# Two feed-forward layers behind clustered attention: the attention's score blocks cut into full 512-column banks, q and k kept in one tile, and the low parts of P and the weight conversions placed anew

## The chip, the cores and the metric

The kernel runs on one core of a Trainium2 chip. A core has five engines that run beside each other and wait for each other through semaphores: TensorE (PE, with PEld for its weight loads), VectorE (DVE), ScalarE (ACT), GpSimd (POOL) and SyncE (SP), which here issues all the transfers. Matmul results land in PSUM, which has eight banks; one bank holds 512 float32 columns on each of 128 partitions. The metric is the device time of one execution in microseconds (us).

## The reference

Attention over 2 batches, 8 heads, 768 positions, head size 64, in which a query sees only the keys of its own cluster; then two feed-forward layers on 1536 rows of 512, inner size 2048.

```python
q_assign = np.argmax(np.einsum('bhsd,hcd->bhsc', q_n, c_n), axis=-1)
k_assign = np.argmax(np.einsum('bhsd,hcd->bhsc', k_n, c_n), axis=-1)
mask = q_assign[:, :, :, None] == k_assign[:, :, None, :]
scores = scale * np.matmul(q, k.transpose(0, 1, 3, 2))
scores = np.where(mask, scores, -1000000000.0)
attn = softmax(scores)                 # max, exp, sum over the last axis
x = np.matmul(attn, v)                 # heads side by side: (1536, 512)
x = softplus(x @ moe_w_in) @ moe_w_out
x = leaky_relu(x @ moe2_w_in) @ moe2_w_out
```

The weights of the feed-forward layers arrive as float64.

## The kernel before, in words

There are 16 heads (8 of batch 0, then 8 of batch 1), and each head's 768 rows make six blocks of 128. Products are made in float16 with a high and a low part: A x B becomes hi x hi + hi x lo + lo x hi.

For one head, in order:

- `load`, `load_v` fetch q, k and v. `split` casts q and k to float16 (`nq`, `nk`), subtracts to get the low parts, and packs both into `n1`, which one transposing transfer turns into `t1`. `split_v` makes the high and low parts of v.
- `assign_mm`, `assign_el` find the cluster of each row: 24 matmuls of 16 columns, then five DVE instructions. ACT writes the one-hot clusters beside the high parts in `nq` and `nk`, and two transfers transpose these into `tq` and `tk`.
- `emit_s1` computes scores to find each query's maximum: per query block two matmuls of 384 columns, each into a bank of its own, and a DVE maximum over each (L250). `emit_m` joins the maxima, writes them into `nq` and has it transposed again (`tm`).
- `emit_s2` computes the scores once more, keys on the partitions, with the maximum subtracted: per key block `kt` two banks of 384 columns, two matmuls each, then the exponential on ACT (L277) into `p`, float32, 128 x 768. A low part `pl` of `p` is subtracted on POOL ("G") or DVE ("D"), as the table `PLO` says by group of heads and key block (L284). Where the table says "P", no low part is made.
- `emit_pv` multiplies P with v. Of a block with a low part, 18 short matmuls: 12 with the high part of P (L311, L312), 6 with `pl` (L316). Of a "P" block, six float32 matmuls (L298).
- `emit_norm` divides by the sum (DVE L345, L346, L348) and writes high and low parts, which are transposed into `xth`, `xtl`.

The feed-forward work (`moe1`) is a generator. Its `layer_in` takes 384 rows at a time and has 16 groups of 12 matmuls (L399); after each group ACT applies softplus twice (L377, L378) and DVE subtracts (L379). `layer_mid` has 16 steps of 12 matmuls (L412). `moe2` does the same with leaky relu, and `layer_out` (L431) ends it. From head 8 on, when the attention of batch 0 is done, `moe_steps` puts eight such steps beside each head.

Weights come in 64 pieces of 512 KB, 32 for each layer pair. `w_piece` issues the transfer into one of two `st` tiles and returns a function that converts it: three DVE instructions on the bits (L137, L140, L143), two on ACT (L147, L148), one on POOL (L149). `w_step` converts one piece and issues the next; it is called from the head loop and once for each step of `moe1`.

The order on each engine comes from the framework's scheduler, which is given a priority for every piece of code (`at_pri`: about the number of the head it belongs to, minus a lead). Every engine then runs its own list in that order. Softplus and the exponential need different ACT tables, so where they alternate, the list has an ACT_TABLE_LOAD in between.

Of the kernel before, what the change touches and what calls it, by code (L numbers as in the profile page):

```python
# [17 lines left out]
BIG = 32768.0  # L18
# [7 lines left out]
}  # L26
NQ_BUFS, NK_BUFS, V_BUFS = (3, 2), (2, 1), 3
# [4 lines left out]
HI = ("AA", "DA", "AA", "AA", "AA", "AA")  # L32
DUP = ("DD", "AA", "AA", "AA", "AA", "AA")
VLO = "GDGDDG"
PLO = ("GPGDGG", "GPGDGG", "GPGDGG", "GPGDGG", "GPPGPP", "GGDGGD")
# [11 lines left out]
def by_group(table, h):  # L47
    return table[min(h // 2, 4 + (h >= 12))]
# [3 lines left out]
def attn_moe_kernel(  # L52
# [50 lines left out]
    xt_h = [const.tile([128, KDM, SEQ], F16, name=f"xth{b}") for b in range(B)]  # L103
    xt_l = [const.tile([128, KDM, SEQ], F16, name=f"xtl{b}") for b in range(B)]
    def padded(bufs, name):
        n, late = sum(bufs), bufs[0]
        tiles = [(acon if i < late else ep).tile([128, C, 128], F16, name=f"{name}_{i}") for i in range(n)]
        return tiles, [tiles[h % n if h < H else (h - H) % late] for h in range(NH)]

    nqs, nq_of = padded(NQ_BUFS, "nq")  # L110
    nks, nk_of = padded(NK_BUFS, "nk")
# [67 lines left out]
    def split_v(h):  # L179
        vv, v2 = v_t.pop(h), v2s[h % V_BUFS]  # L180
        S.copy(out=v2[:, :, D:2 * D], in_=vv)
        ENG[by_group(VLO, h)].tensor_tensor(out=v2[:, :, 0:D], in0=vv, in1=v2[:, :, D:2 * D], op=ALU.subtract)

    def split(h):
        qk = ld_t.pop(h)
        nq, nk = nq_of[h], nk_of[h]
        n1 = atile([128, C, 4, D], F16, "n1", h)
        for t_, n_ in enumerate((nq, nk)):
            (S.copy if by_group(HI, h)[t_] == "A" else V.tensor_copy)(out=n_[:, :, 0:D], in_=qk[:, t_])
            G.tensor_tensor(out=n1[:, :, 1 + t_, :], in0=qk[:, t_], in1=n_[:, :, 0:D], op=ALU.subtract)  # L190
            (S.copy if by_group(DUP, h)[t_] == "A" else V.tensor_copy)(out=n1[:, :, 3 * t_, :], in_=n_[:, :, 0:D])
# [18 lines left out]
    def assign_el(h):  # L210
        nq, nk = nq_of[h], nk_of[h]
# [24 lines left out]
    def emit_s1(h, c):  # L236
        t, tk = tp2[h]
        if c == 0:
            mm_t[h] = atile([128, C, 2], F32, "mm", h)
        for j in range(2):  # L240
            bank = ring("s1", h)
            o = bank[:, 0:3 * 128].rearrange("p (c r) -> p c r", c=3)
            PE.matmul(  # L243
                out=o,
                lhsT=t[0:KS1, c, :],
                rhs=tk[0:KS1, 3 * j:3 * j + 3, :],
                start=True,
                stop=True,
            )
            V.reduce_max(out=mm_t[h][:, c, j:j + 1], in_=bank[:, 0:3 * 128], axis=AX)  # L250

    def emit_m(h):
        nq = nq_of[h]
# [13 lines left out]
    def emit_s2(h, kt):  # L267
        t1 = tp1[h].rearrange("p (c t) r -> p c t r", t=2)
        t2 = tp2[h][1]
        tqh = tpq[h]  # L270
        p = atile([128, 2, 384], F32, "p", h)
        for j in range(2):
            sp = ring("s2", h)[:, 0:384]
            o = sp.rearrange("p (c r) -> p c r", c=3)
            PE.matmul(out=o, lhsT=t1[:, kt, 1, :], rhs=t1[:, 3 * j:3 * j + 3, 0, :], start=True, stop=False)  # L275
            PE.matmul(out=o, lhsT=t2[0:KS2, kt, :], rhs=tqh[0:KS2, 3 * j:3 * j + 3, :], start=False, stop=True)  # L276
            S.activation(out=p[:, j, :], in_=sp, func=AF.Exp, scale=scale)  # L277
        pb = p.bitcast(BF16).rearrange("p a (r t) -> p a r t", t=2)[:, :, :, 1]
# [10 lines left out]
    def emit_pv(h, kt):  # L289
        v2 = v2s[h % V_BUFS]  # L290
        if kt == 0:
            x_t[h] = px.tile([128, 512], F32, tag="x", name="x")
        xps = x_t[h]
        p, pl = p_t.pop((h, kt))
        if pl is None:
            pf = p.rearrange("p a r -> p (a r)")
            for c in range(C):
                PE.matmul(  # L298
                    out=xps[:, c * XW:(c + 1) * XW],
                    lhsT=pf[:, c * 128:(c + 1) * 128],  # L300
                    rhs=v32s[h % V_BUFS][:, kt, :],
                    start=(kt == 0 and c == 0),
                    stop=False,
                )
            return
        pb = p.bitcast(BF16).rearrange("p a (r t) -> p (a r) t", t=2)[:, :, 1]
        pl = pl.rearrange("p a r -> p (a r)")
        for c in range(C):
            cs = slice(c * 128, (c + 1) * 128)
            o = xps[:, c * XW:(c + 1) * XW]  # L310
            PE.matmul(out=o, lhsT=pb[:, cs], rhs=v2[:, kt, D:2 * D + 1], start=(kt == 0 and c == 0), stop=False)  # L311
            PE.matmul(out=o[:, 0:D], lhsT=pb[:, cs], rhs=v2[:, kt, 0:D], start=False, stop=False)  # L312
        for c in range(C):
            cs = slice(c * 128, (c + 1) * 128)
            o = xps[:, c * XW:(c + 1) * XW]
            PE.matmul(out=o, lhsT=pl[:, cs], rhs=v2[:, kt, D:2 * D + 1], start=False, stop=False)  # L316
# [324 lines left out]
```

## Time and profile before

| | |
|---|---|
| median of 3 runs | 817.93 us (815.01 to 820.43) |
| the profiled execution | 823.73 us |
| its span, first to last instruction | 822.0 us |
| PE / PEld busy | 735.4 / 448.0 us |
| DVE / ACT / POOL busy | 413.3 / 386.2 / 228.4 us |
| mean granted TensorE clock | 0.962 of full speed |

Busy time of PE is not PE at its peak: matmuls are pipelined, and the profile's ends of them overlap. Where PE is full, the time from the start of one matmul to the start of the next is what counts.

### The profile page before, as it was taken

Reading aid. Unit: us, or ns where it says so; the run is one execution under the profiler, and the core shown is the slowest. Engines: PE = TensorE matmul, PEld = TensorE weight load, DVE = VectorE, ACT = ScalarE, POOL = GpSimd, SP = SyncE. Lnnn points to the kernel's source line nnn. Section 1 sums busy time; section 2 is a strip of 40 time slices with the busy share of each in tenths; the row PEclk is TensorE's granted clock in tenths of the full one; section 3 lists DMA queues with packets and bytes.
Section 4 is the critical chain, followed back from the end, with each engine's and each line's share of the span. In section 5 each row is a group of like instructions: output and inputs, shape, how many; then the busy total and the mean of one; then the engine's idle time right before and its main releaser. Section 6 shows DMA issues by size and latency. Waiting matters only on the chain.

```text
span 822.0 us, 14081 instructions
## 1 busy us (share of the span) xinstructions
PE 735.4 (89%) x5712; PEld 448.0 (55%) x5712; DVE 413.3 (50%) x790; ACT 386.2 (47%) x797; POOL 228.4 (28%) x192
## 2 busy tenths in 40 slices
PE   1688988798887999998979779999999999999998
PEld 1256656565554675665545446666644644644643
DVE  6899997889687764522778971211200210210210
ACT  3466656479798633497535641412411411411410
POOL 4266757645164443422434340000000000000000
PEclk9999988989879898999999999999999999999999
DMA  7976656685656463101455430000000000000000
GB/s 186 224 172 123 117 119 144 106 203 148 152 145 144 114 110 69 31 1 20 139 157 167 154 102 1 1 1 1 1 14 26 1 14 26 1 13 26 1 14 26
DMA packets 104881, 66.02 MB, mean 80 GB/s; under 512 B 90992, under 2 KB 95088, under 8 KB 104816
## 3 DMA queue, kind: packets, MB, share of 16 engines
q1 hardware_dynamic: 104816, 65.13, 33.2%
q8 instruction: 44, 0.72, 0.4%
q14 instruction: 21, 0.17, 0.1%
HBM read 43.02 MB, written 3.15 MB: 56 GB/s over the span
## 4 chain that ended last, share of the span: by engine, by line
PE 56%; DVE 18%; ACT 11%; DMA 10%; issue 3%; SPq 1%; POOL 0%; ACTq 0%; DVEq 0%; POOLq 0%
PE m L399 21%; PE m L431 15%; PE m L412 10%; DVE mm L250 4%; DVE wc L143 3%; DVE wc L140 3%; DMA st<-in_moe_w_in_dram 3%; DVE wc L137 2%; ACT L377 2%; ACT p L277 2%; PE x L298 2%; DMA tm<-nq 2%; DMA tk<-nk 2%; PE s L275 2%; PE s L243 1%
## 5 line engine op out<-in xcount | busy, mean ns | idle before, releaser
L379 DVE TENSOR_TENSOR g_l<-mr,g_h 128x384 f16<-128x384 f32 x128 | 77.1, 603 | 235.0 <-ACT mr L378 235.0
L284 POOL TENSOR_TENSOR pl<-p 128x768 f16<-128x768 f32 x56 | 89.2, 1599 | 83.1 <-ACT p L277 77.0
L250 DVE TENSOR_REDUCE mm<-s 128x1 f32<-128x384 f32 x160 | 85.5, 549 | 39.3 <-PE s L243 38.5
L377 ACT ACTIVATE g_h<-m 128x384 f16<-128x384 f32 x128 | 62.4, 488 | 88.7 <-PE m L399 88.2
L277 ACT ACTIVATE p<-s 128x384 f32<-128x384 f32 x160 | 75.7, 488 | 52.9 <-PE s L276 49.8
L399 PE MATMUL m<-xth,w_inh 128*128 128x384 f16 x256 | 85.0, 335 | 7.7 <-ACT mr L378 7.7
L412 PE MATMUL m<-g_h,w_outh 128*128 128x384 f16 x256 | 84.9, 332 | 7.7 <-DVE xtl L417 4.9
L412 PE MATMUL m<-g_l,w_outh 128*128 128x384 f16 x256 | 84.9, 332 | 3.7 <-DVE g_l L379 3.7
L399 PE MATMUL m<-xtl,w_inh 128*128 128x384 f16 x256 | 85.3, 334 | 0.0
L412 PE MATMUL m<-g_h,w_outl 128*128 128x384 f16 x256 | 84.9, 332 | 0.0
L399 PE MATMUL m<-xth,w_in2h 128*128 128x384 f16 x256 | 83.3, 326 | 0.0
L399 PE MATMUL m<-xtl,w_in2h 128*128 128x384 f16 x256 | 83.3, 326 | 0.0
L275 PE MATMUL s<-t 128*128 128x384 f16 x160 | 55.9, 351 | 22.3 <-ACT p L277 11.2
L399 PEld LDWEIGHTS <-w_inh 128*128 128x128 f16 x512 | 51.2, 101 | 43.0 <-issue 13.3
L412 PEld LDWEIGHTS <-w_outh 128*128 128x128 f16 x512 | 50.7, 100 | 42.5 <-issue 11.8
L431 PE MATMUL m<-w_out2h,g_h 128*128 128x512 f16 x192 | 72.8, 379 | 0.0
L431 PE MATMUL m<-w_out2l,g_h 128*128 128x512 f16 x192 | 72.8, 379 | 0.0
L431 PE MATMUL m<-w_out2h,g_l 128*128 128x512 f16 x192 | 72.8, 379 | 0.0
L243 PE MATMUL s<-tk,tq 80*128 80x384 f16 x160 | 55.2, 363 | 18.3 <-DVE mm L250 12.5
L399 PEld LDWEIGHTS <-w_in2h 128*128 128x128 f16 x512 | 50.1, 98 | 33.4
L378 ACT ACTIVATE mr<-m 128x384 f32<-128x384 f32 x128 | 62.2, 486 | 0.0
L431 PEld LDWEIGHTS <-g_h 128*128 128x128 f16 x384 | 37.6, 98 | 44.9
(109 smaller groups left out, 1382.0 us busy)
## 6 DMA issues: line engine op xcount, KB each, us to landing
st<-in_moe_w_in_dram SPq DMA_DIRECT2D x32, 512.0 KB, 4.2
st<-in_moe_w_out_dram SPq DMA_DIRECT2D x32, 512.0 KB, 3.6
qk<-in_q_dram SPq DMA_DIRECT2D x16, 192.0 KB, 3.4
qk<-in_k_dram SPq DMA_DIRECT2D x16, 192.0 KB, 3.6
v<-in_v_dram SPq DMA_DIRECT2D x16, 192.0 KB, 3.3
out_dram<-ob SPq DMA_DIRECT2D x12, 256.0 KB, 2.0
t<-n SPq DMA_TRANSPOSE x16, 4.6
tq<-nq SPq DMA_TRANSPOSE x16, 2.9
```

The source lines that it names most:

```text
L140: V.scalar_tensor_tensor(out=c, in0=hi, scalar=-0x40000000, in1=c, op0=ALU.bitwise_and, op1=ALU.bitwise_or)
L243: PE.matmul(out=o, lhsT=t[0:KS1, c, :], rhs=tk[0:KS1, 3 * j:3 * j + 3, :], start=True, stop=True,)
L250: V.reduce_max(out=mm_t[h][:, c, j:j + 1], in_=bank[:, 0:3 * 128], axis=AX)
L275: PE.matmul(out=o, lhsT=t1[:, kt, 1, :], rhs=t1[:, 3 * j:3 * j + 3, 0, :], start=True, stop=False)
L277: S.activation(out=p[:, j, :], in_=sp, func=AF.Exp, scale=scale)
L284: ENG[eng].tensor_tensor(out=pl, in0=p, in1=pb, op=ALU.subtract)
L377: S.activation(out=late["h"][:, m, :], in_=hp, func=func, scale=scale, alpha=alpha)
L378: S.activation(out=r, in_=hp, func=func, scale=scale, alpha=alpha)
L379: V.tensor_tensor(out=late["l"][:, m, :], in0=r, in1=late["h"][:, m, :], op=ALU.subtract)
L399: PE.matmul(out=hp, lhsT=w_, rhs=x_, start=(i == 0), stop=(i == len(ops) - 1))
L412: PE.matmul(out=yp, lhsT=w_[:, kk, ms], rhs=g_[:, kk, :], start=(n == 0), stop=(n == 3 * KFF - 1))
L431: PE.matmul(out=op, lhsT=g_[:, kk, rs], rhs=w_[:, kk, :], start=(n == 0), stop=(n == 3 * KFF - 1))
```

## The change

Score blocks. A pair of 128-row blocks needs 2 x 768 columns; before, that was four banks of 384, now it is three full banks: 512 of the first block, 256 of each, 512 of the second (`PARTS`). A head has nine maxima and nine exponentials in place of twelve each. `emit_s2`, `emit_pv` and `p` work on pairs of key blocks.

q and k share a tile (`nqk`): one cast, one copy and one subtraction of 768 columns in place of two of 384 each, and one transposing transfer `tqk` in place of `tq` and `tk`. High and low parts of the result share `xn` and one transfer.

Low parts. `PLO` is now ("PGP", "GDG") by pair of key blocks, for heads 0 to 7 and 8 to 15: of the first eight heads, four of six key blocks are float32 products (before one of six), and of the others none (before four of six in heads 8 to 11). The low part of v is always POOL's.

Weights. `w_step` is called once for each pair of key blocks from the first head on until 33 have been made, and all 32 pieces of the first layer pair are in its queue from the start.

```diff
-    "p": (3, 2), "pl": (2, 2), "h16": (2, 0), "svt": (2, 0), "svr": (2, 0),
+    "p": (2, 1), "pl": (2, 0), "h16": (2, 0), "svt": (2, 0), "svr": (2, 0),
-NQ_BUFS, NK_BUFS, V_BUFS = (3, 2), (2, 1), 3
+NQK_BUFS, V_BUFS = 3, 3
-PLO = ("GPGDGG", "GPGDGG", "GPGDGG", "GPGDGG", "GPPGPP", "GGDGGD")
+PLO = ("PGP", "GDG")
-FF_PRI, FF_STEP, FF_RATE = 8, 0.25, 1.333
-W_FREE, W_FROM, W_TO, W_PER = 4, 8, 10, 5
-W_PRI = ((0, 0.5), (17, 0.3))
+FF_PRI, FF_STEP, FF_RATE = 8, 0.25, 2.667
+W_FREE, W_FROM, W_TO = 4, 1, 9
+W_PRI = ((0, 0.3), (17, 0.3))
...
-        ENG[by_group(VLO, h)].tensor_tensor(out=v2[:, :, 0:D], in0=vv, in1=v2[:, :, D:2 * D], op=ALU.subtract)
+        G.tensor_tensor(out=v2[:, :, 0:D], in0=vv, in1=v2[:, :, D:2 * D], op=ALU.subtract)
...
+        hi = nqk[:, :, :, 0:D]
+        S.copy(out=hi, in_=qk)
+        S.copy(out=n1[:, :, 0:4:3, :].rearrange("p c t d -> p t c d"), in_=hi)
+        G.tensor_tensor(out=n1[:, :, 1:3, :].rearrange("p c t d -> p t c d"), in0=qk, in1=hi, op=ALU.subtract)
...
+    PARTS = (((0, slice(0, 4)),), ((0, slice(4, 6)), (1, slice(4, 6))), ((1, slice(0, 4)),))
...
+    def emit_s2(h, k0):
...
+        for part in PARTS:
+            bank = ring("s2", h)
+            n = 512 // len(part)
+            for i, (r, blocks) in enumerate(part):
+                o = bank[:, i * n:(i + 1) * n].rearrange("p (c r) -> p c r", r=128)
+                kt = 2 * k0 + r
+                PE.matmul(out=o, lhsT=t1[:, kt, 1, :], rhs=t1[:, blocks, 0, :], start=True, stop=False)
+                PE.matmul(out=o, lhsT=t2[0:KS2, 1, kt, :], rhs=tqh[0:KS2, blocks, :], start=False, stop=True)
...
+        eng = PLO[h // H][k0]
+        pl = None
+        if eng != "P":
...
-            if h < H - 1 and (j + h * C) % W_PER == 0:
+            if 0 < cnt["w"] < 33:
                 w_step()
...
+    wq.extend(out_pieces(w_out1, w_outh, w_outl))
+
     def moe1():
-        wq.extend(out_pieces(w_out1, w_outh, w_outl))
```

In the order of DVE, the first place is the middle of the first eight heads. Before (L256 to L260 join the maxima of head 7; L182 is the low part of v, L284 a low part of P, and the pair of L137 and L140 opens the conversion of two weight pieces):

```order
L182 TENSOR_TENSOR v_1_96<-v_1_99,v_1_96 128x6x64
L250 TENSOR_REDUCE mm<-s_1973 128x1
L250 TENSOR_REDUCE mm<-s_1976 128x1
L256 TENSOR_REDUCE m_1982<-mm 128x6
L137 TENSOR_SCALAR wc<-st 128x512 x2
L257 SCALAR_TENSOR_TENSOR nq_89<-m_1982 128x6
L260 TENSOR_SCALAR nq_89<-m_1982 128x6x2
L284 TENSOR_TENSOR pl<-p 128x768
L140 SCALAR_TENSOR_TENSOR wc<-st,wc 128x512 x2
```

And now, where the maxima of the same head are joined (L254 to L258; L126, L129, L132 are one whole conversion, L354 and L355 end head 5, L204 opens the search for the clusters of a later head):

```order
L254 TENSOR_REDUCE m_1698<-mm 128x6
L255 SCALAR_TENSOR_TENSOR nqk_86<-m_1698 128x6
L258 TENSOR_SCALAR nqk_86<-m_1698 128x6x2
L126 TENSOR_SCALAR wc<-st 128x512
L129 SCALAR_TENSOR_TENSOR wc<-st,wc 128x512
L132 SCALAR_TENSOR_TENSOR wc<-st,wc 128x512
L354 TENSOR_SCALAR dd<-x 128x6
L204 TENSOR_REDUCE mx<-as 128x12
L355 RECIPROCAL dd<-dd 128x6
```

The low parts of v and P have left DVE in these heads, and conversions lie between most of its other work: up to the end of head 7 the list has 31 of them, before 11.

In the order of ACT, the second place is the end of attention, behind the result of head 14 (L350, now L359). Before, softplus (L377, L378) and the exponential (L277) alternate there, with a table load at each turn:

```order
L350 CAST xnh<-y 128x6x64
L377 ACT_TABLE_LOAD
L377 ACTIVATE g_h<-m 128x384
L378 ACTIVATE mr<-m 128x384
L277 ACT_TABLE_LOAD
L277 ACTIVATE p<-s_5701 128x384
L277 ACTIVATE p<-s_5754 128x384
L277 ACTIVATE p<-s_5758 128x384
L377 ACT_TABLE_LOAD
```

Now, behind the result of the same head, the exponentials of the last head (L279, L281) stand in one row, and the first softplus of the second 384 rows (L386, L387) comes after them:

```order
L359 CAST xn<-y 128x6x64
L279 ACTIVATE p<-s_5232 128x512
L281 ACTIVATE p<-s_5236 128x2x256
L279 ACTIVATE p<-s_5242 128x512
L279 ACTIVATE p<-s_5311 128x512
L281 ACTIVATE p<-s_5315 128x2x256
L425 ACTIVATE xt_83<-m 128x384
L279 ACTIVATE p<-s_5321 128x512
L386 ACT_TABLE_LOAD
L386 ACTIVATE g_h<-m 128x384
L387 ACTIVATE mr<-m 128x384
```

The second block of 384 rows starts later against the attention: up to the result of head 15, 25 softplus groups stood in the list, now 18.

## Rows read from the trace of the kernel before

**Rows 1.** Busy time by stretch: start:end, length, engines (instructions), clock, DMA share, GB/s.
```profile
0.00:164.00 164.00, 120.37 (x1542) 83.52 (x1543) 140.13 (x314) 88.49 (x213) 96.01 (x92) 0.94 0.72 149
164.00:273.00 109.00, 91.17 (x692) 61.39 (x691) 88.33 (x154) 94.03 (x169) 51.34 (x40) 0.85 0.64 157
273.00:382.00 109.00, 102.66 (x1100) 69.93 (x1099) 53.97 (x118) 62.83 (x121) 37.67 (x29) 0.97 0.27 54
382.00:482.00 100.00, 85.19 (x511) 49.80 (x509) 77.16 (x112) 55.08 (x109) 38.62 (x30) 0.99 0.48 145
482.00:822.00 340.00, 336.00 (x1874) 183.35 (x1871) 53.69 (x95) 85.75 (x187) 4.76 (x4) 1.00 0.03 12
```

**Rows 2.** Timeline of DVE: the reciprocals that end heads 7, 10 and 15.
```profile
163.73 0.18 DVE L346 RECIPROCAL dd<-dd 128x6 f32<-128x6 f32 x1
...
273.05 0.18 DVE L346 RECIPROCAL dd<-dd 128x6 f32<-128x6 f32 x1
...
381.63 0.18 DVE L346 RECIPROCAL dd<-dd 128x6 f32<-128x6 f32 x1
```

**Rows 3.** The chain that ended last, from 480 us: start, length, what.
```profile
506.48 31.20 PE m L399 x192
...
600.08 31.08 PE m L431 x144
```

**Rows 4.** Groups of DVE, 0 to 164 us: busy, mean ns, idle before and releaser.
```profile
L250 DVE TENSOR_REDUCE mm<-s 128x1 f32<-128x384 f32 x78 | 41.2, 547 | 9.3 <-PE s L243 9.0
...
L143 DVE SCALAR_TENSOR_TENSOR wc<-st,wc 128x512 int32<-128x512 int32 x11 | 11.3, 1034 | 0.0
L284 DVE TENSOR_TENSOR pl<-p 128x768 f16<-128x768 f32 x8 | 11.1, 1391 | 0.6 <-ACT p L277 0.5
L140 DVE SCALAR_TENSOR_TENSOR wc<-st,wc 128x512 int32<-128x512 int32 x11 | 10.9, 1000 | 0.0
...
L182 DVE TENSOR_TENSOR v<-v,v 128x384 f16<-128x384 f32 x6 | 6.4, 1071 | 1.5 <-ACT v L181 1.5
...
L137 DVE TENSOR_SCALAR wc<-st 128x512 int32<-128x512 int32 x11 | 5.1, 479 | 2.9 <-DMA st<-in_moe_w_in_dram 2.8
...
L215 DVE TENSOR_REDUCE mx<-as 128x12 f32<-128x192 f32 x11 | 3.8, 347 | 3.7 <-PE as L202 3.5
```

**Rows 5.** Timeline of DVE: two maxima back to back.
```profile
26.45 1.01 DVE L250 TENSOR_REDUCE mm<-m 128x1 f32<-128x384 f32 x2
```

**Rows 6.** Groups of ACT, whole span: reads of 384 and of 512 columns.
```profile
L277 ACT ACTIVATE p<-s 128x384 f32<-128x384 f32 x160 | 75.7, 488 | 52.9 <-PE s L276 49.8 <-PE x L311 1.5 <-PE x L312 0.2
...
L436 ACT ACTIVATE ob<-m 128x512 f32<-128x512 f32 x12 | 7.2, 597 | 116.5 <-PE m L431 116.5
```

**Rows 7.** Groups of ACT, 164 to 273 us.
```profile
L148 ACT ACTIVATE wc<-wc 128x512 f32<-128x512 f32 x22 | 13.8, 628 | 0.6
L147 ACT ACTIVATE w_outh<-wc 128x512 f16<-128x512 f32 x15 | 9.4, 630 | 4.4 <-DVE wc L143 4.4
```

**Rows 8.** Timeline of ACT: a table load and what follows it.
```profile
191.81 1.28 ACT L277 ACT_TABLE_LOAD   x1
193.10 0.49 ACT L277 ACTIVATE p<-s 128x384 f32<-128x384 f32 x1
```

**Rows 9.** Timeline of PE: six short matmuls, a float32 block, and what starts behind each.
```profile
243.03 1.53 PE L298 MATMUL x<-v,p 128*128 128x65 f32 x12
244.39 0.33 PE L275 MATMUL s<-t 128*128 128x384 f16 x1
...
326.31 0.34 PE L316 MATMUL x<-v,pl 128*128 128x65 f16 x6
326.49 0.33 PE L275 MATMUL s<-t 128*128 128x384 f16 x1
```

**Rows 10.** Groups of DVE, 385 to 480 us.
```profile
L137 DVE TENSOR_SCALAR wc<-st 128x512 int32<-128x512 int32 x28 | 15.9, 566 | 18.4 <-DMA st<-in_moe_w_in_dram 10.4 <-POOL w_in2l L149 3.9 <-DMA st<-in_moe_w_out_dram 2.9
```

**Rows 11.** Waits of the DMA queue: waiter, releaser: us, times, longest.
```profile
SPq L132 <- DVE wc L143: 109.0, 45, 8.2
```

More of the change, by code (lines that the diff above doesn't have):

```diff
@@ L102, in attn_moe_kernel @@
     w_outl = const.tile([128, KFF, DM], F16, name="w_outl")
[L103 to L111, printed above, removed]
+    xts = [const.tile([128, KDM, 2, SEQ], F16, name=f"xt{b}") for b in range(B)]
+    xt_h = [x[:, :, 0, :] for x in xts]
+    xt_l = [x[:, :, 1, :] for x in xts]
+    nqks = [acon.tile([128, 2, C, 128], F16, name=f"nqk_{i}") for i in range(NQK_BUFS)]
     v2s = [acon.tile([128, C, 2 * D + 1], F16, name=f"v2_{i}") for i in range(V_BUFS)]
@@ L239, in emit_s1 @@
+    def emit_s1(h, c0):
+        t = tp2[h]
+        if c0 == 0:
             mm_t[h] = atile([128, C, 2], F32, "mm", h)
-        for j in range(2):
+        mm = mm_t[h]
+        for part in PARTS:
             bank = ring("s1", h)
[L242 to L250, printed above, removed]
+            n = 512 // len(part)
+            for i, (r, blocks) in enumerate(part):
+                PE.matmul(
+                    out=bank[:, i * n:(i + 1) * n].rearrange("p (c r) -> p c r", r=128),
+                    lhsT=t[0:KS1, 0, c0 + r, :],
+                    rhs=t[0:KS1, 1, blocks, :],
+                    start=True,
+                    stop=True,
+                )
+            if len(part) == 1:
+                c = c0 + part[0][0]
+                V.reduce_max(out=mm[:, c, 0:1], in_=bank, axis=AX)
+            else:
+                V.reduce_max(out=mm[:, c0:c0 + 2, 1:2], in_=bank.rearrange("p (c n) -> p c n", c=2), axis=AX)
@@ L287, in attn_moe_kernel, with emit_pv @@
     XW = D + 1
-    def emit_pv(h, kt):
+    def emit_pv(h, k0):
         v2 = v2s[h % V_BUFS]
-        if kt == 0:
+        if k0 == 0:
             x_t[h] = px.tile([128, 512], F32, tag="x", name="x")
         xps = x_t[h]
-        p, pl = p_t.pop((h, kt))
-        if pl is None:
-            pf = p.rearrange("p a r -> p (a r)")
-            for c in range(C):
[L298 to L316, printed above, removed]
@@ new lines, in emit_pv @@
+        p, pl = p_t.pop((h, k0))
+        for r in range(2):
+            kt = 2 * k0 + r
+            if pl is None:
+                for c in range(C):
+                    PE.matmul(
+                        out=xps[:, c * XW:(c + 1) * XW],
+                        lhsT=p[:, r, c * 128:(c + 1) * 128],
+                        rhs=v32s[h % V_BUFS][:, kt, :],
+                        start=(kt == 0 and c == 0),
+                        stop=False,
+                    )
+                continue
+            pb = p.bitcast(BF16).rearrange("p k (r t) -> p k r t", t=2)[:, r, :, 1]
+            for c in range(C):
+                cs = slice(c * 128, (c + 1) * 128)
+                o = xps[:, c * XW:(c + 1) * XW]
+                PE.matmul(out=o, lhsT=pb[:, cs], rhs=v2[:, kt, D:2 * D + 1], start=(kt == 0 and c == 0), stop=False)
+                PE.matmul(out=o[:, 0:D], lhsT=pb[:, cs], rhs=v2[:, kt, 0:D], start=False, stop=False)
+            for c in range(C):
+                cs = slice(c * 128, (c + 1) * 128)
+                o = xps[:, c * XW:(c + 1) * XW]
+                PE.matmul(out=o, lhsT=pl[:, r, cs], rhs=v2[:, kt, D:2 * D + 1], start=False, stop=False)
@@ L552, in chain @@
             with at_pri(h - LEAD_MAX):
-                for c in range(C):
+                for c in range(0, C, 2):
                     emit_s1(h, c)
@@ L580, in attn_moe_kernel @@
             emit_sv(h)
-        for j in range(C):
-            with at_pri(h + j / 6):
+        for j in range(C // 2):
+            with at_pri(h + j / 3):
                 emit_s2(h, j)
```

93 lines of the change are left out of this document (41 added, 52 removed), and 4 rows, old and new, of the table BUFS.

## The prediction

> **What bounds the kernel now.** I read the stretches first, to see where TensorE is full and where another engine is. The last 340 us are plain: PE is busy 336 of 340 us at full clock, and the chain that ended last is made there of runs of 192 matmuls in 31.20 us (0.1625 us each) and of 144 in 31.08 us [rows 1, 3]. Nothing that the change touches is in there. So the question is how much time passes before, and how much feed-forward work is left then.
>
> Until 164 us, when head 7 ends [rows 2], DVE is busy for 140.1 us of 164, PE for 120.4, ACT for 88.5, POOL for 96.0 [rows 1]. DVE is the bound of this first stretch, with 23.9 us idle, of which the largest item is 9.3 us before the score maxima [rows 4]. From 164 to 273 us (head 10 ends) ACT is the fullest, 94.0 of 109 us, DVE next with 88.3 [rows 1]: here the softplus of the first 384 rows, the table loads and 20 of the weight conversions come together. From 273 to 382 us (head 15 ends) it is PE, 102.7 of 109 [rows 1]. From 382 to 482 us DVE has 77.2 of 100 us busy with the second layers' conversions, and PE loses time to them.
>
> **The account.** TensorE's busy time overlaps itself, so I count its work by starts: 0.1625 us for 384 columns [rows 3]; six short matmuls take 0.18 us, 0.030 each; a float32 block of six (12 records) 1.36 us to the next start [rows 9], against 18 x 0.030 = 0.54 us for a block with a low part. In the order of before, 300 of the 1536 L399 matmuls and all 192 L412 of the first 384 rows precede the end of head 15. What remains is 1236 + 576 of 0.1625 us and four runs of 31.08 us: 294.5 + 124.3 = 418.8 us. From 381.6 to 822.0 us there are 440.4, so 21.6 us are lost after head 15, in the stretch of the second conversions. In the new order 216 precede it, so 84 x 0.1625 = 13.6 us more remain: 432.4 us. The conversions still pending there (30) and the code that paces them, one for each feed-forward step, are unchanged, so I keep 21.6 us of loss: 454.0 us after head 15. What is left is when head 15 ends.
>
> **First stretch, DVE.** Maxima: the order has 110 up to the end of head 7, now 84. Two of 384 columns take 1.01 us and one alone 0.547 [rows 4, 5], so each next one adds 0.46. For 512 columns the bounds are 0.46 (all of it fixed) and 0.62 (all of it by columns); ACT's reads grow by 0.109 us for the same 128 columns [rows 6], which would give 0.57. I take 0.60: 84 x 0.60 = 50.4 against 110 x 0.46 = 50.6, so nothing is gained where the change's main idea lies; at 0.46 it would be 12 us. Low parts: eight of P at 1.391 and six of v at 1.071 leave DVE, -11.1 and -6.4 us [rows 4]. Conversions: 31 in place of 11, 20 x (1.034 + 1.000 + 0.479) = +50.3 us [rows 4]. The sum is +32.6, DVE 172.7 us. Idle was 23.9; 3.5 of it was an early wait for the first clusters [rows 4] into which two conversions now fall, so 20.4 stay. Head 7 ends at 193 us, 29 later. Bounds: idle at 5 % of the stretch (172.7 / 0.95 = 182) below; above, each conversion waiting for its transfer as in the second conversions, 18.4 us for 28 [rows 10], 0.66 each: +17.5 us after the 2.9 already there [rows 4], 210.
>
> The other engines have room there. PE: 24 more float32 blocks, each 1.36 - 0.54 = 0.82 us dearer, add 19.7 us to 120 of busy time in a stretch of 193. POOL loses half of its low parts of P and gains 20 conversions; ACT gains 40 conversion passes of 0.63 us, 25 us on 88.5, and stays under 120. The merged cast, copy and subtraction are the same columns in fewer instructions, and the transposes the same bytes: I cost both at nothing, covered by DVE's backlog, and a few us if that cover is gone, since a head's first cast now waits for q and k together.
>
> **Second stretch, ACT.** In the new order all 16 softplus groups are done by the end of head 11, before by the end of head 10, so I compare 164 to 273 us with four heads of the new kernel. ACT: 24 loads for 22, 2 x 1.29 = +2.6; one conversion in place of 20, 19 x 1.26 = -23.9 [rows 7]; 36 reads of 512 for 36 of 384, 36 x 0.109 = +3.9 [rows 6]; a fourth head's casts and small steps, 3 us. That is -14.4, so 79.6 us busy. Of 15 idle, 4.4 were waits for DVE's conversions [rows 7], which go: 90 us. PE's own work there is 350 matmuls of 384 columns on average (158 of scores, 192 of the feed-forward) and 607 short ones, 56.9 + 18.2 = 75.1 us; in the third stretch PE reached 0.90 of its time (next part), which makes 83. I take 88, between the two, and 80 to 96 as bounds.
>
> A table load takes 1.28 us here, and the next ACTIVATE starts 1.29 after the load did [rows 8]. The Trainium skill ("ScalarE: Activation LUTs", What ACT_TABLE_LOAD costs) adds a drain of about 1.38 us to each switch, about 2.66 in all; by it, the two further loads would cost 5.3 us in place of 2.6, and this stretch 2.7 us more. The trace shows no such drain between load and use, and 22 switches of 2.66 us beside the rest would not fit into the 109 us.
>
> **Third stretch, PE.** Before, 453 matmuls of 384 columns, 618 short ones and four float32 blocks: 73.6 + 18.5 + 5.4 = 97.5 us in 109, a share of 0.90. Now 317, 528 and none: 51.5 + 15.8 = 67.3, at the same share 75 us, bounds 71 and 80. Part of that is work put off (the 13.6 us counted above), the rest is the head by which the new order is ahead, and the float32 blocks of heads 8 to 11 that are gone. The 12 table loads that leave this stretch were not the bound there: ACT 62.8 us of 109 [rows 1].
>
> **Sum.** Head 15 ends at 193 + 88 + 75 = 356 us, 25.6 earlier; 13.6 of it are given back behind: 12.0 us less than the profiled execution, whose span is 822.0 us and whose time was 823.73. The median of the runs is 817.93, so 806.
>
> **Rivals.** (a) Conversions are free work, and fill DVE's gaps: head 7 at 182 us, and the second stretch at PE's 83. That is another 16 us: 790. For it: DVE's idle before the maxima is a wait for PE, which other work can cover. Against: every engine runs its list in a fixed order, and a conversion in front of a maximum can as well delay it.
> (b) Feeding the conversions holds up attention, and the kernel is slower than before. SP runs its list in order too, a weight transfer waits there for a free `st` (109.0 us in 45 waits, 2.4 each [rows 11]), and behind it stand the transposes for which heads wait. With 0.66 us for each conversion (17.5 us) and a third of 20 further waits of 2.4 us on transposes (16 us), the first stretch takes 33 us more: 839. It decides from 12 us of such stalls on. For it: DMA is busy 0.72 of the first stretch already [rows 1], and 20 pieces more go in. Against: a piece came every 3 us in the second conversions, here every 6.
> (c) The float32 blocks lie on the path: the product of a head has one bank, and the next head waits for it. Then the 19.7 us of the first stretch show in full: 826. Against: PE has 70 us to spare there; for it, TensorE's waits come in bursts. The Trainium skill ("FP8 and Floating Point Precision", TensorE Precision Notes) says that true float32 is four passes; four times 0.030 us for six matmuls would be 0.72 us a block, and 24 blocks only 4.3 us dearer. The trace, with 1.36 us to the next start, is above that [rows 9].
>
> **How the numbers follow.** The forecast gets 0.45, (a) 0.25, (b) 0.15, (c) 0.15. About 1 % (810 to 826) is what a measurement of this kernel can tell from no change. The forecast's own bounds run from 792 to 820 and put two thirds of it under 810: 0.31; with (a) 0.56 for faster. The rest of the forecast, (c) and the weak end of (b) make 0.30 for the same, and 0.14 stays for slower. The range leaves out most of (b) and the far end of (a): 788 to 826.
>
> **What would show it.** Right, if the end of head 7 lies near 193 us with DVE above 0.85 busy, heads 8 to 15 take some 163 us in place of 218, 32 conversions are done before the softplus gets dense, and the last 340 us look the same. A maximum of 512 columns near 0.60 us from the one before settles the first term. Wrong, if DVE's waits for weight transfers before head 7 exceed 10 us, if PE waits for the transposes of q and k there, or if PE's loss after head 15 is not near 22 us.

## The result and the profile after

The changed kernel is slower by 1.2 %: 829.0 us (median of 19 runs, 824.4 to 834.5) against 819.1 us (19 runs, 815.0 to 829.9), a ratio of 1.012 with an interval of 1.010 to 1.015. Forecast were 806 us, faster, and a range of 788 to 826. The ratios in this document leave out executions more than 1.5 % above the fastest of their kernel: three of the six of e1 (842.6 to 846.0 us), elsewhere at most one.

The profiled execution of the changed kernel took 824.95 us, 4 below its median; that of before, 823.73 us, 5 above. So the two traces differ by 1.1 us where the medians differ by 10, and a stage of one trace is good to a few us. Nearly the same list of instructions up to head 7 ran three times under the profiler (the changed kernel, and two experiments: e9, which splits one transfer of every second head, and e14, which moves feed-forward steps): head 7 ended at 200.0, 207.4 and 203.7 us.

The view of stretches, cut at the ends of heads 7, 11 and 15 (columns as in [rows 1]):

```profile
0.00:200.02 200.02, 159.18 (x1403) 114.03 (x1404) 161.82 (x321) 107.93 (x210) 99.60 (x90) 0.89 0.76 177
200.02:303.08 103.06, 85.54 (x955) 55.77 (x954) 58.58 (x115) 83.32 (x135) 46.44 (x35) 0.93 0.39 80
303.08:371.63 68.55, 68.15 (x840) 46.70 (x839) 33.36 (x68) 29.39 (x59) 25.02 (x19) 1.00 0.29 55
...
472.00:823.00 351.00, 346.45 (x1940) 189.50 (x1938) 58.11 (x102) 90.47 (x200) 5.20 (x4) 1.00 0.03 12
```

The ends themselves, in the timeline of DVE (as [rows 2]):

```profile
200.02 0.18 DVE L355 RECIPROCAL dd<-dd 128x6 f32<-128x6 f32 x1
303.08 0.18 DVE L355 RECIPROCAL dd<-dd 128x6 f32<-128x6 f32 x1
371.63 0.19 DVE L355 RECIPROCAL dd<-dd 128x6 f32<-128x6 f32 x1
```

Before, heads 7, 11 and 15 ended at 163.7, 295.0 and 381.6 us. So the first stretch is 36 us longer, the four heads behind it take 103 us where they took 131, the last four 69 where they took 87, and 451.5 us are left (span 823.1) where 440.4 were. In the first stretch neither DVE (0.81 of it busy) nor PE (0.80) is full; before, DVE was at 0.85 and PE at 0.73. The chain at the end is the one of [rows 3]:

```profile
757.18 31.20 PE m L408 x192
788.38 31.09 PE m L440 x144
```

Groups of DVE from 20 to 200 us (as [rows 4]; L126, L129 and L132 are the conversion, L246 and L248 the maxima):

```profile
L132 DVE SCALAR_TENSOR_TENSOR wc<-st,wc 128x512 int32<-128x512 int32 x29 | 26.9, 935 | 0.3
L129 DVE SCALAR_TENSOR_TENSOR wc<-st,wc 128x512 int32<-128x512 int32 x29 | 24.8, 862 | 0.3
L246 DVE TENSOR_REDUCE mm<-s 128x1 f32<-128x512 f32 x32 | 21.8, 683 | 6.7 <-PE s L237 6.6
...
L126 DVE TENSOR_SCALAR wc<-st 128x512 int32<-128x512 int32 x29 | 16.4, 574 | 10.1 <-DMA st<-in_moe_w_in_dram 5.7 <-DMA st<-in_moe_w_out_dram 2.8 <-POOL w_outl L138 1.4
```

A conversion takes 0.935 + 0.862 + 0.574 = 2.37 us of DVE (2.51 were put in). Two maxima of 512 columns in a row take 1.27 us and one 0.68 (as [rows 5]), so the next one adds 0.59:

```profile
74.70 1.27 DVE L246 TENSOR_REDUCE mm<-m 128x1 f32<-128x512 f32 x2
77.11 0.69 DVE L246 TENSOR_REDUCE mm<-s 128x1 f32<-128x512 f32 x1 [0.28 <-PE s L237]
```

Groups of PE, 0 to 200 us:

```profile
L308 PE MATMUL x<-v,p 128*128 128x65 f32 x384 | 54.8, 297 | 0.2 <-DVE y L357 0.2
L237 PE MATMUL s<-tqk 80*128 80x512 f16 x33 | 16.9, 516 | 15.2 <-DMA tqk<-nqk 9.2 <-DVE mm L246 5.8
...
L276 PE MATMUL s<-t 128*128 128x512 f16 x25 | 11.6, 465 | 15.2 <-DMA t<-n 14.1 <-ACT p L279 1.1
```

The 384 float32 records are 32 blocks. PE waits 9.2 us for the joint transpose of q and k (before, 6.3 for that of k). The 14.1 us for that of `n1` are a single wait, at the very start, before the first matmul of head 0 (before, 11.1). How a wait for DVE and the float32 blocks meet shows in 5-us windows, and in the timeline of PE there:

```profile
105.00:110.00 5.00, 3.99 (x43) 2.73 (x39) 4.28 (x7) 3.70 (x8) 3.96 (x3) 1.00 1.07 179
110.00:115.00 5.00, 2.17 (x16) 0.92 (x13) 5.00 (x8) 3.12 (x8) 4.34 (x5) 0.65 0.62 192
115.00:120.00 5.00, 4.99 (x19) 3.35 (x18) 4.91 (x10) 1.19 (x2) 1.55 (x2) 0.50 1.10 231
120.00:125.00 5.00, 5.00 (x43) 3.21 (x43) 3.75 (x8) 3.10 (x6) 1.59 (x2) 0.50 0.37 109
125.00:130.00 5.00, 5.00 (x48) 4.29 (x47) 4.60 (x9) 2.30 (x4) 1.02 (x2) 0.99 0.38 84
```

```profile
92.82 1.45 PE L308 MATMUL x<-v,p 128*128 128x65 f32 x12
94.10 0.38 PE L276 MATMUL m<-t 128*128 128x512 f16 x1
...
112.66 1.18 PE L237 MATMUL s<-tqk 80*128 80x512 f16 x3 [1.99 <-DVE mm L246]
114.67 0.58 PE L237 MATMUL m<-tqk 80*128 80x512 f16 x1 [0.83 <-DVE mm L246]
...
117.78 2.66 PE L308 MATMUL x<-v,p 128*128 128x65 f32 x12
120.23 0.26 PE L320 MATMUL x<-v,p 128*128 128x65 f16 x1
```

From 110 to 115 us PE is busy for 2.17 us, waiting for DVE, which is full; the granted clock then is 0.50, the lower of its two levels (1.2 of 2.4 GHz), for ten microseconds in which PE is full. A float32 block takes 1.28 us to the next start at full clock and 2.45 us at half. So in this place each engine is late in turn: DVE while conversions and the search for clusters stand in front of maxima, then PE. The clock falls without such a wait too, as at 166 us, where PE has been full (PE alone, clock, DMA share, GB/s):

```profile
160.00:165.00 5.00, 5.00 (x58) 1.00 0.95 204
165.00:170.00 5.00, 5.00 (x40) 0.66 0.84 188
```

The Trainium skill ("FP8 and Floating Point Precision", TensorE Precision Notes) gives true float32 four passes. An estimate from that and the short matmuls of before is 0.72 us a block. The two blocks here, 1.28 and 2.45 us, do not agree with that estimate, as [rows 9] did not.

### The profile page after: what moved, and what is told of

It is laid out like the page before. It is cut to its first block, busy times and chain, and to the rows that moved or that the text cites. A ratio compares the mean times of both kernels' runs of the same rounds, so it can differ in the third digit from the quotient of the medians.

```text
span 823.1 us, 13681 instructions
## 1 busy us (share of the span) xinstructions
PE 748.7 (91%) x5664; PEld 458.5 (56%) x5664; DVE 393.1 (48%) x715; ACT 366.6 (45%) x713; POOL 214.2 (26%) x176
## 4 chain that ended last, share of the span: by engine, by line
PE 57%; DVE 16%; DMA 13%; ACT 9%; issue 3%; SPq 1%; POOL 1%; DVEq 0%; ACTq 0%; POOLq 0%
PE m L408 20%; PE m L440 15%; PE m L421 10%; DMA st<-in_moe_w_in_dram 5%; DVE wc L129 4%; DMA st<-in_moe_w_out_dram 3%; DVE wc L132 3%; DMA tqk<-nqk 3%; DVE wc L126 2%; PE x L308 2%; DVE mm L246 2%; PE s L237 2%; PE s L276 2%; PE s L277 2%; ACT L279 1%
## 5 line engine op out<-in xcount | busy, mean ns | idle before, releaser
L408 PE MATMUL m<-xt,w_inh 128*128 128x384 f16 x512 | 97.0, 327 | 11.4 <-ACT mr L387 11.4
L386 ACT ACTIVATE g_h<-m 128x384 f16<-128x384 f32 x128 | 62.6, 490 | 90.7 <-PE m L408 90.5
L293 POOL TENSOR_TENSOR pl<-p 128x768 f16<-128x768 f32 x48 | 73.9, 1547 | 94.6 <-ACT p L281 72.3
L408 PE MATMUL m<-xt,w_in2h 128*128 128x384 f16 x512 | 93.6, 326 | 0.0
L276 PE MATMUL s<-t 128*128 128x512 f16 (+1 forms) x168 | 57.7, 353 | 24.2 <-DMA t<-n 14.1
L408 PEld LDWEIGHTS <-w_inh 128*128 128x128 f16 x512 | 49.4, 98 | 44.6 <-issue 13.9
L237 PE MATMUL s<-tqk 80*128 80x512 f16 (+1 forms) x168 | 52.2, 385 | 20.1 <-DMA tqk<-nqk 10.4
L387 ACT ACTIVATE mr<-m 128x384 f32<-128x384 f32 x128 | 62.6, 489 | 0.0
L246 DVE TENSOR_REDUCE mm<-s 128x1 f32<-128x512 f32 x72 | 48.8, 684 | 22.2 <-PE s L237 22.0
L445 ACT ACTIVATE ob<-m 128x512 f32<-128x512 f32 x12 | 7.2, 597 | 116.3 <-PE m L440 116.3
L277 PE MATMUL s<-tm,tqk 81*128 81x512 f16 (+1 forms) x168 | 58.2, 359 | 0.5 <-DMA tm<-nqk 0.5
L132 DVE SCALAR_TENSOR_TENSOR wc<-st,wc 128x512 int32<-128x512 int32 x64 | 57.0, 895 | 1.2
```

The costliest lines, as they stand in the source:

```text
L132: V.scalar_tensor_tensor(out=c, in0=lo, scalar=29, in1=c, op0=ALU.logical_shift_right, op1=ALU.bitwise_or)
L237: PE.matmul(out=bank[:, i * n:(i + 1) * n].rearrange("p (c r) -> p c r", r=128), lhsT=t[0:KS1, 0, c0 + r, :], rhs=t[0:KS1, 1, blocks, :], ...
L246: V.reduce_max(out=mm[:, c, 0:1], in_=bank, axis=AX)
L276: PE.matmul(out=o, lhsT=t1[:, kt, 1, :], rhs=t1[:, blocks, 0, :], start=True, stop=False)
L277: PE.matmul(out=o, lhsT=t2[0:KS2, 1, kt, :], rhs=tqh[0:KS2, blocks, :], start=False, stop=True)
L293: G.tensor_tensor(out=pl[:, r], in0=p[:, r], in1=pb[:, r], op=ALU.subtract)
```

## The experiments

Two theories stand against each other first. P: the float32 blocks hold up the first stretch on PE's list. F: the conversions of the new weight schedule hold it up on DVE. Each comparison is with runs of the kernel before on the same chip. "Head 7", "11", "15" are the ends of these heads in the profiled execution, in us.

**Undoing the weight schedule, the float32 share, or putting each into the kernel before (e1 to e4).** e1 is the changed kernel with

```diff
-W_FREE, W_FROM, W_TO = 4, 1, 9
+W_FREE, W_FROM, W_TO, W_PER = 4, 8, 10, 5
-            if 0 < cnt["w"] < 33:
-                w_step()
+            for kt in (2 * j, 2 * j + 1):
+                if h < H - 1 and (kt + h * C) % W_PER == 0:
+                    w_step()
```

(with `W_PRI` and the place where the second half of the pieces is queued as before). e3 is the kernel before with the new schedule, one call for every second key block. e2, the changed kernel without float32 blocks, and e4, the kernel before with as many as the changed one, differ in a table:

```diff
-PLO = ("PGP", "GDG")
+PLO = ("GDG", "GDG")
...
-PLO = ("GPGDGG", "GPGDGG", "GPGDGG", "GPGDGG", "GPPGPP", "GGDGGD")
+PLO = ("PPGGPP", "PPGGPP", "PPGGPP", "PPGGPP", "GGDDGG", "GGDDGG")
```

> The changed kernel with the weight schedule of before: pieces called for every fifth key block, 11 conversions up to the end of head 7 in place of 31. Theory F (feeding: the added conversions and their transfers hold up the first stretch and the transfer of head 7's result): head 7 ends under 175 us in place of 200, and the time falls to 805 to 820 us. Theory P (the float32 blocks load TensorE in the first stretch and let its clock fall): the first stretch stays near 190 us, time within 5 us of 829. Theory B (full banks and joint transposes make each head slower): within 5 us of 829.

> The changed kernel without float32 blocks: the low parts of all pairs of heads 0 to 7 are made, two pairs on POOL and one on DVE, as in heads 8 to 15. Theory P: TensorE's first stretch loses 32 blocks of 1.36 us or more and its clock stays up; time falls by 10 to 20 us to 809 to 819. Theory F: within 5 us of 829, or slower, since DVE gets 8 low parts of 2 us back. Theory B: within 5 us of 829.

> The kernel before with the new weight schedule alone: 27 conversions up to the end of head 7 in place of 11. Theory F: slower than before by 10 us or more, 829 to 845, head 7 ends 35 us later or more. Theory P and theory B: within 5 us of 819; my prediction's account of DVE alone would have head 7 end 40 us later and the later stretches give back most of it.

> The kernel before with the new share of float32 blocks alone: four of six key blocks of heads 0 to 7, none in heads 8 to 15. Theory P: slower than before by 10 us or more, with a first stretch at a granted clock under 0.88. Theory F and theory B: within 5 us of 819, or faster, since DVE loses 8 low parts of 1.4 us in the first stretch and TensorE 16 blocks in the second.

| | ratio, interval | head 7 / 11 / 15 | DVE, PE busy up to head 7 |
|---|---|---|---|
| e1 | 1.012 (1.005 to 1.018) | 189.9 / 307.6 / 378.9 | 112, 154 |
| e2 | 1.024 (1.020 to 1.029) | 213.8 / 313.8 / 383.0 | 192, 137 |
| e3 | 1.031 (1.026 to 1.037) | 201.8 / 312.6 / 400.1 | 182, 142 |
| e4 | 1.037 (1.031 to 1.043) | 187.6 / 320.2 / 402.4 | 124, 150 |

The waits of e4 from 20 to 187 us and of e1 from 20 to 190 us show what the first stretch then hangs on:

```profile
DVE mm L250 <- PE s L243: 35.7, 24, 4.3
```

```profile
DVE mm L246 <- PE s L237: 36.6, 17, 5.7
```

DVE, at 0.66 and 0.59 of its time, waits for scores that stand behind float32 blocks on PE; before, it waited 9.0 us for them [rows 4]. In e4 24 more blocks end head 7 by 23.8 us later, 1.0 us each: they are on the path in full, as P says, though the clock of the stretch is 0.91 and not under 0.88. Where DVE is the bound (e3, and e2, whose low parts of P go to DVE and POOL), F holds: 182 us of work end at 202. So each shift alone costs the kernel before 3 % or more, and taking either out of the changed kernel alone does not make it faster.

**Leaving the low part of P out of the float32 blocks (e5, e6).** e5 is the changed kernel with twelve short float16 matmuls on the high part of P in place of each float32 block; e6 is that with the old weight schedule.

```diff
-                        lhsT=p[:, r, c * 128:(c + 1) * 128],
-                        rhs=v32s[h % V_BUFS][:, kt, :],
+                    PE.matmul(out=o, lhsT=pb[:, cs], rhs=v2[:, kt, D:2 * D + 1], ...)
+                    PE.matmul(out=o[:, 0:D], lhsT=pb[:, cs], rhs=v2[:, kt, 0:D], ...)
```

> The changed kernel; the blocks that were float32 products are multiplied by the high part of P alone (12 short float16 matmuls in place of six float32 ones), so the low part of P is left out there; DVE, POOL and ACT have the same work. Theory P (float32 blocks on TensorE, with the clock that falls around them, hold up the first stretch): head 7 ends at 180 us or earlier in place of 200, and the time falls by 15 us or more, to 814 or less. Theory B (full banks and joint transposes): head 7 still near 195 to 200, time within 5 us of 829.

> As the run before, with the weight schedule of before as well, so that neither float32 blocks nor the added conversions load the first stretch (the low part of P is left out in four of six blocks of heads 0 to 7). Theory P: head 7 ends at 160 us or earlier (the old schedule with float32 blocks: 190). Theory B: 175 us or later, with no engine over 0.75 busy.

e5: 0.998 (0.996 to 1.000), heads at 169.7 / 291.6 / 360.7. e6: 0.998 (0.996 to 1.000), heads at 152.3 / 290.8 / 360.8. Their first stretches:

```profile
0.00:169.66 169.66, 118.34 (x1395) 75.67 (x1396) 147.22 (x292) 99.76 (x197) 87.08 (x83) 0.86 0.83 187
```

```profile
0.00:152.33 152.33, 107.54 (x1394) 69.89 (x1395) 112.47 (x247) 82.98 (x169) 69.75 (x70) 0.96 0.79 163
```

Against the 200 to 207 us of the changed kernel the first stretch loses 30 to 38 us; against e1, with the same 112 us of DVE work, e6 loses 37.5, 1.2 us a block. But the time falls by 12 only: both end head 11 at 291, wherever head 7 ended. So a first stretch shorter than some 170 us buys nothing further behind it.

**Banks, joint tiles and transfers alone (e7), and the two shifts without them (e8).** e7 is the changed kernel with the old schedule (the lines of e1) and the old `PLO`, asked per key block; e8 is the kernel before with the new schedule and the table of e4.

```diff
-        eng = PLO[h // H][k0]
+        engs = by_group(PLO, h)[2 * k0:2 * k0 + 2]
...
+            for r in range(2):
+                if engs[r] != "P":
+                    ENG[engs[r]].tensor_tensor(out=pl[:, r], in0=p[:, r], in1=pb[:, r], op=ALU.subtract)
```

> The changed kernel with the weight schedule and the table of low parts of before, chosen by single key blocks: full banks, the joint tile of q and k, the joint transposes and the smaller pools are what is left of the change (and the low part of v on POOL). Theory P: as fast as before or faster, 805 to 822 us, head 7 at 165 or earlier. Theory B: 829 or slower, head 7 at 175 or later.

> The kernel before with the new weight schedule and the new share of float32 blocks, but with its 384-column banks, separate tiles and old pools. If the two shifts are all that costs time, it is as slow as the changed kernel or slower, 829 to 850, head 7 at 195 to 205: DVE busy 10 us less than with the new weights alone (182 us), TensorE longer. If the joint tiles and banks are what makes the two shifts bearable (each shift alone cost more without them), it is slower than 850.

e7: 1.009 (1.005 to 1.013), heads at 173.0 / 298.3 / 366.7. Its first stretch:

```profile
0.00:172.98 172.98, 129.45 (x1565) 89.27 (x1566) 142.52 (x275) 90.99 (x182) 101.40 (x88) 0.89 0.67 149
```

e8: 1.039 (1.033 to 1.045), heads at 206.1 / 330.2 / 418.9. The rewritten attention costs about 8 us by itself. By the ratios, each shift alone and both together cost 26 to 32 us in the kernel before, and together 2 us, within the intervals, in the rewritten one. With a median of 853 us e8 bears out the second reading of its text: the rewritten attention makes the two shifts bearable.

**The fourth corner, half of the float32, and two transfers (e10, e11, e9).** e10 is e7 with the new schedule left in; e11 makes the edit of e5 for `r == 1` alone, the second block of each pair; e9 has

```diff
-            nc.sync.dma_start_transpose(
-                out=xts[b][:, hh // 2].rearrange("p l (c r) -> p (l c) r", c=C),
-                in_=xn.rearrange("p l c d -> p (l c d)"),
-            )
+            for l in range(2):
+                nc.sync.dma_start_transpose(
+                    out=xts[b][:, hh // 2, l].rearrange("p (c r) -> p c r", c=C),
+                    in_=xn[:, l].rearrange("p c d -> p (c d)"),
+                )
```

> The changed kernel with the normalised result's high and low parts transposed by two transfers, as in the kernel before, instead of one. Theory L (the second stretch of the changed kernel starts late because one joint transfer waits for the low part, which POOL makes 4.5 us after the high part): the first feed-forward matmul comes 4 to 6 us sooner after head 7, head 11 ends at 298 us instead of 303, and the time is about 825. Rival N (every group of feed-forward matmuls needs the low part at its second matmul, so the high part alone starts nothing): the first feed-forward matmul moves by at most 3 us, the stretch from head 7 to head 11 stays at 100 us or more, time 827 to 831.

> The changed kernel with the old table for the low parts of P (per key block: 8 float32 blocks in heads 0 to 7, the rest on DVE and POOL) but the new weight schedule. It is the fourth corner: changed kernel 829, old weights 838, old weights and old table 828. Theory A (the two costs add up): 829 + 828 - 838 = 819, head 7 near 185 us. Theory F (DVE pays for whatever TensorE no longer does: with a conversion more per step DVE is over 0.9 busy): DVE 180 us busy by head 7, head 7 at 198 us or later, time 830 or more.

> The changed kernel in which one of the two key blocks of each float32 pair is done with float16 matmuls on the high part of P alone (its low part is left out), so 16 float32 blocks instead of 32 before head 7 ends and 4 short ones less each. All of them left 829 with head 7 at 200; none left 817 with head 7 at 170. Theory P (each block has its price on the path, about 1 us): half way, head 7 at 185 us, time 823. Rival C (the cost comes with TensorE's clock, which falls once a head has gaps, not with the number of blocks): head 7 within 5 us of one of the two ends, clock of the first stretch 0.82 to 0.86 as in both.

The second text takes 838 us for e1; by its ratio e1 stands at 828. e10: 1.015 (1.009 to 1.021), head 7 at 204.5 with DVE 182 us busy: theory F.

```profile
0.00:204.51 204.51, 146.08 (x1563) 98.30 (x1564) 181.74 (x322) 105.86 (x207) 126.11 (x104) 0.83 0.70 164
```

The four corners of the rewritten kernel (e7 1.009, e1 1.012, e10 1.015, as changed 1.012) lie within their intervals. e11: 1.011 (1.005 to 1.018), head 7 at 191.4, head 11 at 300.7. Half of the blocks takes 9 to 16 us off the first stretch, and more than half of that is gone by head 11; the time does not tell the two theories apart. e9: 1.010 (1.003 to 1.018), 100.5 us from head 7 to head 11, the first softplus 20.0 us behind head 7 instead of 22.3: rival N. What stands in that gap shows in the timeline of the changed kernel:

```profile
204.36 3.19 POOL L293 TENSOR_TENSOR pl<-p 128x768 f16<-128x768 f32 x2
207.51 1.60 POOL L138 TENSOR_TENSOR w_outl<-wc,w_outh 128x512 f16<-128x512 f32 x1
209.07 0.91 POOL L360 TENSOR_TENSOR xn<-y,xn 128x384 f16<-128x384 f32 x1
...
212.25 1.81 SPq L182 DMA_TRANSPOSE t<-n  x1
214.11 3.06 SPq L365 DMA_TRANSPOSE xt<-xn  x1
...
218.88 0.85 PE L408 MATMUL m<-xt,w_inh 128*128 128x384 f16 x2
...
220.99 1.28 ACT L386 ACT_TABLE_LOAD   x1
222.28 0.49 ACT L386 ACTIVATE g_h<-m 128x384 f16<-128x384 f32 x1
```

The low part of head 7's result stands on POOL behind two low parts of P and a conversion, then its transfer on SP behind another one.

**Fewer float32 blocks in the kernel before (e12, e13).** Of its 24 blocks, e12 moves the 16 of heads 8 to 11 to POOL, e13 the other eight too:

```diff
-PLO = ("GPGDGG", "GPGDGG", "GPGDGG", "GPGDGG", "GPPGPP", "GGDGGD")
+PLO = ("GPGDGG", "GPGDGG", "GPGDGG", "GPGDGG", "GGGGGG", "GGDGGD")
```

> The kernel before with one line changed: the low parts of P in heads 8 to 11, of which four key blocks in six were float32 blocks on TensorE (16 blocks), all go to POOL, as float16 low parts. Theory P (each float32 block costs its 0.8 to 1 us on the path wherever TensorE has little slack): 13 to 16 us less in the stretch from head 7 to head 11, which has TensorE 113 of 131 us busy, and 805 us. POOL gets 16 low parts of 1.69 us, 27 us on 60.5 of 131, and stays under 90. Rival S (that stretch is set by ScalarE, 104 of 131 us busy with the softplus groups and its table loads, or by POOL's low parts that now come late): head 11 stays within 5 us of 295, and the time is 815 to 823.

> The same, and in heads 0 to 7 the one float32 block of each head goes to POOL as well, so that no low part of P is left to TensorE's float32. Theory P: 8 blocks of 0.8 to 1 us less on TensorE in the first stretch, but there DVE is the bound and POOL gets 8 more of 1.62 us on 96 of 164: head 7 at 157 to 164, the time 0 to 7 us under that of the other. Rival S: POOL becomes late in the first stretch, head 7 at 168 or more, and the time 820 or more.

e12: 1.003 (1.000 to 1.006), head 11 at 294.0: rival S; ACT is 106 of 134 us busy there, and POOL's low parts wait 21.7 us for exponentials. e13: 1.014 (1.010 to 1.018), head 7 at 179.9. Float32 blocks cost a microsecond each only where the first stretch hangs on PE, and a POOL or DVE that makes the low part can cost as much.

**As much feed-forward ahead of head 15 as before (e14, e15).** e14 is the changed kernel, e15 is e7, each with

```diff
-FF_PRI, FF_STEP, FF_RATE = 8, 0.25, 2.667
+FF_PRI, FF_STEP, FF_RATE = 8, 0.2, 2.667
```

> The changed kernel with the distance between feed-forward steps in the order 0.2 of a head instead of 0.25, so that 300 instead of 216 first-layer matmuls precede the end of head 15, as in the kernel before (and 60 instead of 12 second-layer ones precede the end of head 11). Theory W (work is only moved): head 15 ends 10 to 14 us later, about 438 us are left behind it, the time is 826 to 832. Rival H (the steps put off in the changed kernel could have filled TensorE's gaps in heads 8 to 11, which is 85 of 103 us busy): head 15 at most 7 us later, the time 815 to 822.

> The same for the changed kernel with the old weight schedule and the old shares of the low parts (828 us with 216 matmuls ahead, head 15 at 366.7): banks, joint tiles and transfers alone, with as much feed-forward ahead of the end of head 15 as before. Theory W: 826 to 831, so the banks and joint tiles by themselves cost 8 us wherever the steps stand. Rival H: 813 to 820, so that the 8 us are the steps put off.

e14: 1.015 (1.010 to 1.019), heads at 203.7 / 309.6 / 390.0. e15: 1.018 (1.012 to 1.023), heads at 182.3 / 319.9 / 399.8. Third stretch of e14:

```profile
309.56:390.03 80.47, 76.00 (x877) 51.43 (x876) 36.88 (x72) 49.95 (x84) 25.42 (x19) 0.98 0.23 46
```

Theory W, and rather more than it: with 84 matmuls (13.6 us) put back ahead, the third stretch of e14 takes 11.9 us more and 9.1 us less is left behind it (442.4 us); by the ratios e14 is 2 us above the changed kernel, within the intervals, and e15 7 us above e7. Softplus and exponentials alternate in that stretch again: ACT has 50 us in it instead of 29, and PE falls from 0.99 busy to 0.94. So what the change puts off is no cost, and rather a gain; with the steps placed as before, the rewritten attention alone is at 1.018, 14.5 us.

## Why the prediction was wrong

Three steps failed: that PE "has 70 us to spare" and so hides the float32 blocks, that the joint tiles and transposes cost nothing, "covered by DVE's backlog", and the second stretch, the term of the sum that missed by most (15 us), whose idle time was put at 10 us and was 20.

**What held.** A maximum of 512 columns came at 0.59 us after the one before (0.60 taken). ACT has 24 table loads of 1.283 us and 83.3 us of work from head 7 to head 11 (79.6 put in). After head 15 there were 451.5 us (454.0). The end is as it was. Where DVE keeps its low parts of P, the account of DVE holds as well: with 11.1 us of them back the forecast's sum is 204 us for e10, and its head 7 ended at 204.5.

**First stretch, DVE.** Forecast 193 us, bounds 182 to 210; it was 200 to 207, within them, but by another way. DVE had 162 us of work, not 172.7, and was idle 38 us, not 20.4; a quarter of that was for weight transfers (8.5 us from 20 us on, against a mark of 10). Two of the signs speak against the forecast: DVE is 0.81 busy, under the mark of 0.85, and PE waits 9.2 us for the transposes of q and k. The step that failed is that PE has 70 us to spare and hides 24 more float32 blocks: e1 and e4 show them on the path with DVE at 0.6 of its time, 1.0 us each, and e5 and e6 take 30 to 38 us off the stretch. e10 shows the same from the other side: it gives 24 of the blocks back to DVE and POOL, DVE has 20 us more work, and head 7 ends within the spread of the three traces above. So what DVE gained by the blocks was lost again. That is rival (c). Its price, 0.82 us by [rows 9], was for a block that runs at full clock; PE runs part of the stretch at half of it (mean 0.89, before 0.94), where a block is 2.45 us. e1 and e7, without the added conversions, are at 0.89 too, so why the clock falls stays open.

**Merged tiles at nothing.** "Covered by DVE's backlog" failed too: e7 and e15, with DVE's work nearly as before (143 and 141 us, before 140), end head 7 at 173 and 182 us instead of 164. Some 3 us of that are there from the start, since PE's first matmul waits 14.2 us for the joint `n1` and waited 11.1. For the rest, from 20 us on in e7 (`as` holds the scores of the cluster search, `svt` a step of the sums of v):

```profile
ACT p L284 <- PE x L312: 9.5, 6, 3.5
...
DVE mx L209 <- PE as L196: 6.5, 3, 3.3
...
DVE svr L343 <- ACT svt L342: 4.0, 3, 1.8
```

The first of these is exponentials that stand until the product of an earlier pair frees its `p` (e15: 11.5 us): P is now held in three pairs, before in five single blocks. That this coarser hold is the cause is argued and not shown. In the changed kernel this wait is 2.8 us only (L308), and before, exponentials waited 19.5 us for scores, which in e7 are 11.9. The other two are waits of DVE, together 0.3 us before in the same part; DVE is idle 30.5 us of its stretch in e7, before 23.8. No run separates the full banks, the joint tile of q and k, the larger `p` and the low part of v on POOL, so the part that costs the 0.9 % stays open.

**Second stretch.** Forecast 88 us, bounds 80 to 96; it was 103, and 100 to 106 in e9 and e14. From the first softplus on the account is right: 80.8 us with ACT 0.88 busy. What it lacked is the 22 us ahead of it, in which the result of head 7 goes through POOL, SP, the transposes and PE, and ACT has 12.5 us of other work:

```profile
200.02:222.28 22.26, 17.90 (x201) 11.20 (x200) 18.05 (x34) 12.53 (x25) 14.53 (x11) 0.77 0.70 160
222.28:303.08 80.80, 67.64 (x760) 44.57 (x757) 40.53 (x82) 70.79 (x111) 31.91 (x25) 0.98 0.31 58
```

Before, the same gap was 16.6 us (163.7 to 180.3), and a stretch cut at the end of head 7 contained it unseen. The idle of 10 us that I allowed should have been 20.

**Third stretch.** Forecast 75 us, bounds 71 to 80; it was 68.6: the 67.3 us of work counted there filled 0.98 of it and not 0.90. That this is due to the tables, which no longer alternate, fits e14: there they do, and PE is 0.94 busy instead of 0.99.

**The sum.** 7 + 15 - 6 - 2.5 us make 13 more than forecast, 823 instead of 810 for the span. The rest of the way to 829 is the choice of executions: the forecast took 6 us off because the profiled execution of before lay above its median, and that of the changed kernel lay 4 below.

**Rivals.** (a) did not happen: conversions did not fill gaps, they lengthened the first stretch (e3, +38 us). (b) is a part: waits of PE for the transposes of q and k and of DVE for weight transfers are some 9 us longer than before there, but the old schedule in the rewritten kernel (e1) gives the same time, so it doesn't decide. (c) is what the first stretch shows; that its 826 us lie near the 829 is luck, since that stretch was only 7 to 14 us over the forecast, not 19.7, and the second made up the rest. What decides the sign is that the rewritten attention by itself is 0.9 % slower, and the two shifts give nothing back in it.

**What stays open.** Why head 11 does not end before 291 us (before, e5, e6, e12: 291 to 295 us with head 7 from 152 to 170): no engine is over 0.85 busy up to there. No kernel here beat the one before: the best, e5, leaves part of the computation out and is level with it.

## What to carry to other kernels

Two engines at 0.8 of a stretch that feed each other are not two engines with a fifth to spare: before work goes to one of them as hidden, take from the trace what the other waits for it now, and price the work in full if they take turns. Cut a stretch where its bounding work really begins, not where the work before ends. Fewer, wider instructions on fewer, larger tiles save little where the cost goes by columns, and what else comes with them can cost more than they save.

## What the runs showed of the hardware

A float32 block of six 65-column matmuls took 1.28 us at full clock and 2.45 at half. The granted clock fell to half in the first stretch once behind a wait of PE (2.17 of 5 us busy from 110 to 115 us) and stayed there for ten microseconds in which PE was full, so that this wait was paid again by the work behind it; from 160 to 170 us it fell while PE was full. From the start of a table load to that of the next ACTIVATE there was 1.29 us again (220.99 to 222.28). The Trainium skill ("ScalarE: Activation LUTs", What ACT_TABLE_LOAD costs) counts about 2.7 us for a switch with its drain. By an estimate from that, 24 of these beside the 52 us of ACT's other work from head 7 to head 11 would be 117 us in a stretch of 103, so the trace does not agree.
